# Loads of weights in parts of 112, 8 and 8 rows, in a decoder of grouped-query attention and a token mixer

## The chip, the cores and the metric

The kernel runs on one core of a Trainium2 chip. The metric is the device time of one execution in microseconds. The program is in float32 throughout, and nearly all of what it does is to stream a key and a value cache from HBM through the on-chip memory, twice over, once for each layer.

## The reference

Two layers, each of attention over a cache and of a mixer over the token axis, for two sequences of one new token. Cut to what matters:

```python
B, Sq, D = 2, 1, 512
Hq, Hkv, Sk, Dh = 32, 8, 32768, 128

def A(x, k_cache, v_cache, wq, wo):
    q = (x @ wq).reshape(B, Sq, Hq, Dh).transpose(0, 2, 1, 3)
    k = repeat(k_cache, Hq // Hkv, axis=1); v = repeat(v_cache, Hq // Hkv, axis=1)
    p = softmax(einsum("bhqd,bhkd->bhqk", q, k) * Dh ** -0.5)
    o = einsum("bhqk,bhkd->bhqd", p, v)
    return o.transpose(0, 2, 1, 3).reshape(B, Sq, Hq * Dh) @ wo

def Bmix(x, w1, b1, w2, b2):        # w1: (1, 1792), w2: (1792, 1)
    h = layernorm(x)
    u = gelu(einsum("bsd,sf->bdf", h, w1) + b1)
    return (einsum("bdf,fs->bds", u, w2) + b2).transpose(0, 2, 1)

x = A_x
for _ in range(2):                  # both layers read the same cache and weights
    x = x + A(layernorm(x), k_cache, v_cache, wq, wo)
    x = x + Bmix(layernorm(x), w1, b1, w2, b2)
```

## The kernel before

The work is cut into 32 units: layer, sequence and key head (`units`). A unit has eight chunks of 4096 keys and eight of values; a chunk is 2 MB, 16 KB in each of 128 rows (partitions). One large tile, `mem`, has thirteen cells of a chunk each. Eight of them take the stream of K and V in turn, mostly four chunks at a time (8 MB per load, 64 KB per row); in the middle of the program, where some of the last head's K and V stay on the chip for the second layer (`KEPT`, `KEPT_K`), the stream runs through three to six cells with loads of one or two chunks. Four cells, from `WCELL0` on, take weights.

The weights of a key head, its columns of `wq` and its rows of `wo` side by side, are one cell: 128 rows of 16 KB, 2 MB (`wqo[h]`). `load_weights(h, cell)` (L101) loads them with one DMA on the SP queue (L103). It is called thirteen times: once at the start for head 0, once for each of the heads 1 to 7 in the first layer, and again for the heads 0 to 4 in the second, since heads 5 to 7 (`RESIDENT`; the last of them is `keeper`) keep their cells.

All loads of K, V and weights are issued from SP, in the order that the kernel plans by hand. `stream` is a list of all loads of K and V, sorted by the chunk at which they are due; `run(t)` issues what is planned with `at(t, ...)` after chunk `t`. The weights of a unit `n` are planned ten chunks before its first chunk of K:

```python
        if n and (units[n] == (0, 0, h) or h in passing and units[n] == (1, 0, h)):
            at(kbeg[n] - 10, load_weights, h, (again if layer else weight_cell)[h])
```

They are read first by `make_q` (L238), four chunks later, and then by `out_2` (L442) after the unit's last chunk of V. A load of K (`load_k`, L272) or V (`load_v`, L352, and L346 for what stays) waits until TensorE has used up what stood in its cells: `k_chunk` (L287) computes the scores of a chunk, `v_chunk` (L391) the sum over its values. The exponentials are ACT's, the maxima and the transposes DVE's. After the last chunk of V comes a tail (`last_out`, `last_mixer`) that ends with a store of the last sequence's row in four pieces (L602); the other sequence's row is stored earlier, from ACT's queue.

Of the kernel before, what the change touches and what calls it, by code (L numbers as in the profile page):

```python
# [13 lines left out]
P = 128  # L14
# [10 lines left out]
KEPT_K = {2: 9, 4: 7, 5: 8}  # L25
KEPT = {2: (8, 6), 4: (8, 3), 5: (3, 13), 6: (8, 4), 7: (8, 5)}
REST = 3
RESIDENT = (5, 6, 7)
PIECES = (32, 16, 8, 4, 4)
THIN = 8  # L30
# [7 lines left out]
def gqa_mixer_kernel(ctx: ExitStack, tc: tile.TileContext, x, kt, v, wqo, cols, out):  # L38
# [16 lines left out]
    nc = tc.nc  # L55
# [31 lines left out]
    heads = list(range(HKV))  # L87
    passing = [h for h in heads if h not in RESIDENT]
    home = {}
    mem = const.tile([P, (WCELL0 + WCELLS) * CK + REST * QT * DH], F32, name="mem")  # L90

    def cells(k, m=1):
        return mem[:, k * CK : (k + m) * CK]
# [4 lines left out]
    def wo_at(h):  # L98
        return cells(home[h])[:, W:].rearrange("p (t c) -> p t c", t=R)

    def load_weights(h, cell):  # L101
        home[h] = cell
        nc.sync.dma_start(cells(cell), wqo[h])  # L103


    used = [0] * (WCELL0 + WCELLS + 1)
# [7 lines left out]
    def buffer(m, limit):  # L114
# [3 lines left out]
        return cells(k, m)  # L118

    load_weights(0, WCELL0)  # L120
    cols_sb = const.tile([P, 3 * FT + 1], F32, name="cols_sb")
    nc.scalar.dma_start(cols_sb, cols)
# [60 lines left out]

    *ends, keeper = RESIDENT
    assert keeper == HKV - 1 and LAYERS == 2 and B == 2
# [17 lines left out]
    def row_tile():  # L203

        return S[HALVES - 1]
# [17 lines left out]
    def unit_of(n):  # L223

        return units[n]
# [451 lines left out]
    kbeg, k_done, vbeg, v_done, t = {}, {}, {}, {}, 0  # L677
# [7 lines left out]
    def at(time, f, *a, rank=1):  # L685
        done.setdefault(time, []).append((rank, f, a))

    HC = NCH // HALVES
    weight_cell = {h: WCELL0 + h % WCELLS for h in heads}
    again = dict(zip(passing, (WCELL0 + k for k in (0, 3, 1, 2, 0))))  # L690
    for n in range(NU):
        layer, b, h = unit_of(n)
        kend, vend = k_done[n, NCH - 1], v_done[n, NCH - 1]
        ahead = v_done[n - 1, NCH - 1] if n else 0
        urgent = n in (N1, N2, NU - 1)
        if n:
            if n in (N1 + 3, N2 + 3):
                q0, q1, q2 = kbeg[n] - 1, kbeg[n] - 1, kbeg[n]
            else:
                q0 = kbeg[n] - (10 if n in (N1 + 2, N2 + 2) else 6)  # L700
                q1, q2 = q0 + 1, q0 + 2
            at(q0, make_q, n, 0)
            at(q1, make_q, n, 1)
            at(q2, make_q, n, 2)
        if n and (units[n] == (0, 0, h) or h in passing and units[n] == (1, 0, h)):
            at(kbeg[n] - 10, load_weights, h, (again if layer else weight_cell)[h])
        at(kend + 1, max_1, n)
        at(kend + 2, max_2, n)
        at(max(k_done[n, HC - 1], v_done[n - 1, HC - 1] if n else 0), turn_scores, n, 0)
        at(kend + 2, exponentials, n, 0)  # L710
        t1 = max(kend + 2, ahead + (2 if urgent else 4))
        at(t1, turn_scores, n, 1)
        at(t1, exponentials, n, 1)
        at(t1 + (1 if n == NU - 1 else 2), denominators, n)
        if n == NU - 1:
            at(t1 + 1, gelu_table)
            at(t1 + 1, last_rows, (layer, b))
            at(vend, last_out, n)
            at(vend, last_mixer, n)
            continue  # L720
        assert vbeg[n + 1] >= vend and (n + 2 >= NU or vbeg[n + 1] > vend)
        at(min(vend + 1, vbeg[n + 1]), out_1, n)
        at(vend + 2, out_2, n)
        if units[n] == lay[layer, b][-1]:
            key = (layer, b)
            at(vend, mix_1, key)
            at(vend + 2, take_rows, key, row_tile())
            at(vend + 3, mix_2, key)
            at(vend + 1, gelu_table)

            when = [vend + 3 + f for f in range(FT + 1)]
            when = [w + (w >= max(k_done[n + 1, NCH - 1] + 2, vend + 4)) for w in when]
            for f, w in enumerate(when):

                if f:
                    at(when[f - 1] + 1, hidden_out, key, f - 1, rank=0)
                if f < FT:
                    at(w, hidden_tile, key, f, rank=2)
            e = when[FT]
            at(e, take_rows, key, None, rank=2)  # L740
            at(e + 1, mix_4, key)
            if layer + 1 < LAYERS:
                at(e + 2, to_columns, key)
                assert e + 2 < kbeg[n + 3]
# [72 lines left out]
```

## Time and profile before

| | |
|---|---|
| runs of the kernel | 2515.88 us median of 3 (2515.83 to 2517.79) |
| profiled execution | 2515.91 us, its span 2514.1 us |
| PE busy | 1498.0 us (60%) |
| DVE, ACT busy | 193.1 us, 198.6 us (8% each) |
| granted TensorE clock, mean | 0.785 |
| moved by DMA | 1071.46 MB in 34802 packets, mean 426 GB/s |
| loads of weights (L103) | 13, of 2048 KB, 33.2 us from issue to landing (median) |

Engines: PE is TensorE, DVE VectorE, ACT ScalarE, POOL GpSimd, and SP the engine that issues the loads; a name with a q at its end (SPq) is the engine's sequencer, which waits and issues. L103 is line 103 of the kernel. The page gives each engine's busy time, the queues of the DMA engines with their packets and the share of sixteen engines' time that those took, and the chain of work that ended last. A load's landing is when all engines that carried it have reported.

### The profile page before, as it was taken

What the parts mean: (1) busy time and instruction counts of PE and PEld (TensorE: products, weight loads), DVE (VectorE), ACT (ScalarE), POOL (GpSimd) and SP (SyncE); (2) the same over time, 40 slices, a digit from 0 to 9 for tenths busy, and PEclk for the clock granted to TensorE, in tenths of its full rate; (3) what the DMA queues carried; (4) which work ended last, traced back from release to release, by engine and by line L of the source; (5) the groups of instructions that cost most, each with busy time, mean ns of one, the idle gap of its engine ahead of it and who ended that gap; (6) DMA issues with size and microseconds to landing.
All of it is one profiled execution on the core that took longest, in us unless ns stands there. A gap on an engine that the chain in (4) does not pass through costs nothing.

```text
span 2514.1 us, 21143 instructions
## 1 busy us (share of the span) xinstructions
PE 1498.0 (60%) x9700; PEld 413.6 (16%) x9700; DVE 193.1 (8%) x494; ACT 198.6 (8%) x582; POOL 4.9 (0%) x17
## 2 busy tenths in 40 slices
PE   4556554565546556677667676555555555566656
PEld 1111111111111111111111121111111111111112
DVE  1000000000000000011001010000000000010002
ACT  0000000000000000021000200000000000012002
POOL 0000000000000000000000000000000000000000
PEclk8777777777777778888898898777777777778878
DMA  9999999999999999999999999999999999999996
GB/s 418 434 434 431 434 432 431 433 431 437 430 431 429 432 429 430 426 421 425 427 426 427 425 421 428 433 435 435 432 433 429 432 432 433 432 430 423 432 432 280
DMA packets 34802, 1071.46 MB, mean 426 GB/s; under 512 B 4117, under 2 KB 4121, under 8 KB 4762
## 3 DMA queue, kind: packets, MB, share of 16 engines
q1 hardware_dynamic: 34424, 1070.09, 99.1%
q8 instruction: 76, 1.25, 0.2%
q14 instruction: 12, 0.10, 0.0%
q10 hardware_dynamic: 290, 0.03, 0.0%
HBM read 1070.10 MB, written 0.00 MB: 426 GB/s over the span
## 4 chain that ended last, share of the span: by engine, by line
DMA 72%; PE 27%; DVE 0%; issue 0%; ACT 0%; ACTq 0%; SPq 0%
DMA mem<-in_kt_dram 60%; PE scores L287 19%; DMA mem<-in_v_dram 12%; PE acc L391 3%; PE misc L238 3%; PE misc L429 1%; PE rows L442 1%; ACT mem L595 0%; PE misc L250 0%; PE rows L610 0%; PE misc L212 0%; ACT mem L584 0%; DVE hid L247 0%; DVE hid L365 0%; PE bcast L633 0%
## 5 line engine op out<-in xcount | busy, mean ns | idle before, releaser
L287 PE MATMUL scores<-mem,qpad 128*32 128x512 f32 x4096 | 648.1, 734 | 565.1 <-DMA mem<-in_kt_dram 564.6
L391 PE MATMUL acc<-mem,S 128*16 128x512 f32 x4092 | 618.2, 734 | 386.7 <-DMA mem<-in_v_dram 379.8
L287 PEld LDWEIGHTS scores<-mem,qpad 128*32 128x32 f32 x4096 | 142.2, 127 | 964.6 <-DMA mem<-in_kt_dram 630.1
L324 ACT ACTIVATE S<-S,neg 128x128 f32<-128x128 f32 x256 | 131.6, 518 | 1997.9 <-DVE neg L315 1524.3
L391 PEld LDWEIGHTS acc<-mem,S 128*16 128x16 f32 x4092 | 133.2, 109 | 737.2 <-issue 577.0
L238 PE MATMUL misc<-mem,xnT 128*1 128x512 f32 x256 | 122.0, 601 | 2.6 <-issue 1.6
L297 DVE TENSOR_REDUCE mx<-scores 128x1 f32<-128x512 f32 x64 | 44.3, 692 | 873.1 <-PE scores L287 853.4
L319 DVE STREAM_TRANSPOSE S<-scores 128x512 f32<-128x512 f32 x64 | 45.5, 711 | 166.8 <-PE acc L391 166.8
L621 ACT ACTIVATE hid<-bcast,bias,scale 128x512 f32<-128x512 f32 x42 | 32.7, 778 | 272.0 <-PE rows L610 136.7
L250 PE MATMUL misc<-one,hid 1*128 1x1 f32 x256 | 34.2, 250 | 33.3 <-DVE hid L247 33.3
L610 PE MATMUL rows<-hid,cols_sb 128*1 128x512 f32 x84 | 50.6, 688 | 4.1 <-ACT hid L621 4.1
L324 ACT ACTIVATION_READ_ACCUMULATOR S<-S,neg 128x1 f32 x256 | 47.8, 187 | 0.0
L429 PEld LDWEIGHTS misc<-selg,S 128*128 128x128 f32 x248 | 35.9, 223 | 44.6 <-issue 42.8
L250 PEld LDWEIGHTS misc<-one,hid 1*128 1x128 f32 x256 | 31.6, 190 | 60.6 <-DVE hid L247 48.2
L429 PE MATMUL misc<-selg,S 128*128 128x4 f32 x248 | 38.6, 279 | 0.9 <-DVE S L426 0.9
L442 PE MATMUL rows<-mem,oT 128*1 128x512 f32 x248 | 38.9, 687 | 0.0
L238 PEld LDWEIGHTS misc<-mem,xnT 128*1 128x1 f32 x256 | 21.5, 85 | 91.1 <-issue 89.9
L437 DVE TENSOR_TENSOR oT<-misc,rl 128x4 f32<-128x4 f32 x31 | 5.0, 162 | 318.3 <-PE misc L429 318.3
L426 DVE COPY S<-acc 128x512 f32<-128x512 f32 x31 | 21.4, 690 | 102.7 <-PE acc L391 102.7
L247 DVE COPY hid<-misc 1x512 f32<-1x512 f32 x32 | 21.5, 671 | 91.5 <-PE misc L238 91.5
L307 DVE TENSOR_REDUCE m<-misc 1x4 f32<-1x128 f32 x32 | 8.9, 279 | 229.6 <-PE misc L305 221.0
L422 DVE RECIPROCAL rl<-misc 128x4 f32<-128x4 f32 x32 | 5.8, 183 | 258.5 <-PE misc L420 258.5
(110 smaller groups left out, 209.9 us busy)
## 6 DMA issues: line engine op xcount, KB each, us to landing
mem<-in_kt_dram SPq DMA_DIRECT2D x60, 2048.0 KB, 12.6
mem<-in_v_dram SPq DMA_DIRECT2D x53, 2048.0 KB, 12.7
mem<-in_v_dram SPq DMA_DIRECT2D x9, 4096.0 KB, 32.5
mem<-in_kt_dram SPq DMA_DIRECT2D x7, 4096.0 KB, 28.2
mem<-in_wqo_dram SPq DMA_DIRECT2D x13, 2048.0 KB, 33.2
mem<-in_v_dram SPq DMA_DIRECT2D x4, 1280.0 KB, 21.0
mem<-in_v_dram SPq DMA_DIRECT2D x2, 768.0 KB, 23.3
mem<-in_v_dram SPq DMA_DIRECT2D x1, 1024.0 KB, 27.4
```

The source lines that it names most:

```text
L238: nc.tensor.matmul(q_ps[n][:1, :], xnT[layer, b][:, d : d + 1], wq_at(h)[:, d, :], start=(d == 0), stop=(d == DT - 1),)
L247: nc.vector.tensor_copy(q_row[n][:1, :], q_ps[n][:1, :])
L250: nc.tensor.matmul(pt[:, r : r + 1], q_row[n][:1, r * DH : (r + 1) * DH], one[:1, :], start=True, stop=True)
L287: nc.tensor.matmul(sc_ps[n, half][32 * g : 32 * g + 32, :], q, kc[:, (k * NG + g) * w : (k * NG + g + 1) * w], start=(i == 0 and k == 0), ...
L297: nc.vector.tensor_reduce(mx[n][:, half : half + 1], sc_ps[n, half], axis=AX.X, op=ALU.max)
L319: nc.vector.transpose(S[half], sc_ps[n, half])
L324: nc.scalar.activation(s[:, :, h], s[:, :, h], AF.Exp, bias=neg[n][:, h : h + 1], scale=SCALE, accum_out=lsum[n][:, half, h : h + 1],)
L391: nc.tensor.matmul(acc[32 * g : 32 * g + R * QT, :], S[half][:, col : col + R * QT], (own if q < stay else vc)[:, q * w : (q + 1) * w], st ...
L429: nc.tensor.matmul(po[:, :R], asb[:, t * DH : (t + 1) * DH], selg[:, t * R : (t + 1) * R], start=(t == 0), stop=(t == QT - 1),)
L442: nc.tensor.matmul(rows[b][32 * r : 32 * r + 1, :], oT[n][:, r : r + 1], wo_at(h)[:, r, :], start=(units[n] == lay[layer, b][0]), stop=(un ...
L610: nc.tensor.matmul(rows[key[1]][32 * g : 32 * g + 1, :], w2c[:, f : f + 1], hid[key, f], start=(f < NG), stop=(f >= FT - NG),)
L621: nc.scalar.activation(hid[key, f], px[key], AF.Gelu_apprx_tanh, bias=shift[key][:, f : f + 1], scale=slope[key][:, f : f + 1],)
```

## The change

`load_weights` takes a list of cuts, and loads the rows between each two of them with a DMA of its own. With `CUTS` these are the rows 0 to 111, 112 to 119 and 120 to 127, so that a load of weights becomes three. The planned loads use `CUTS`, but for the keeper's; the first one, of head 0 before everything else, has the default and stays whole. So eleven of the thirteen are cut: heads 1 to 6 in the first layer and 0 to 4 in the second. By the words given with the change, eight of the sixteen DMA engines then get nine rows and eight get seven, instead of eight each.

```diff
+CUTS = (0, 112, 120, 128)
...
-    def load_weights(h, cell):
+    def load_weights(h, cell, cuts=(0, P)):
         home[h] = cell
-        nc.sync.dma_start(cells(cell), wqo[h])
+        for p0, p1 in zip(cuts, cuts[1:]):
+            nc.sync.dma_start(cells(cell)[p0:p1], wqo[h, p0:p1])
...
         if n and (units[n] == (0, 0, h) or h in passing and units[n] == (1, 0, h)):
-            at(kbeg[n] - 10, load_weights, h, (again if layer else weight_cell)[h])
+            at(kbeg[n] - 10, load_weights, h, (again if layer else weight_cell)[h], (0, P) if h == keeper else CUTS)
```

Nothing else of the kernel is changed, and no other engine's instructions are.

## The prediction

> **What bounds the kernel now.** I began with the page's span, transfer and queue lines, then a table of stages, then the chain that ended last.
>
> ```profile
> span 2514.1 us, 21143 instructions
> ...
> DMA packets 34802, 1071.46 MB, mean 426 GB/s; under 512 B 4117, under 2 KB 4121, under 8 KB 4762
> ## 3 DMA queue, kind: packets, MB, share of 16 engines
> q1 hardware_dynamic: 34424, 1070.09, 99.1%
> q8 instruction: 76, 1.25, 0.2%
> ...
> q10 hardware_dynamic: 290, 0.03, 0.0%
> ...
> DMA 72%; PE 27%; DVE 0%; issue 0%; ACT 0%; ACTq 0%; SPq 0%
> ```
>
> The sixteen DMA engines are busy for 99% of the span, nearly all of it with q1, SP's loads. The table by stage (each row ends with the granted clock, the DMA share and GB/s) says that this holds in each stage and not only on average:
>
> ```profile
> 100.00:500.00 400.00, 225.39 (x1470) 63.90 (x1470) 25.14 (x64) 21.47 (x80) 0.00 (x0) 0.74 1.00 433
> 900.00:1250.00 350.00, 237.52 (x1462) 61.30 (x1458) 30.09 (x77) 37.06 (x97) 1.09 (x2) 0.84 1.00 426
> 2050.00:2480.00 430.00, 254.38 (x1662) 71.55 (x1658) 32.36 (x82) 45.99 (x119) 0.54 (x1) 0.77 1.00 430
> ```
>
> TensorE works 225 of 400 us there and otherwise waits. So the time is what the busiest DMA engine has to do, plus the tail after the last load. Whatever lengthens every load's slowest engine lengthens the kernel one for one; a microsecond on an engine that is ahead costs nothing until it is no longer ahead.
>
> The price of a row: 433 GB/s over sixteen engines is 27.1 GB/s for each, so 16 KB, one row of a weight, takes 0.605 us, and the eight rows that an engine has of such a load take 4.84 us.
>
> **The sixteen engines are not equally loaded.** The page says that 76 packets of instructions, 16 KB each, go through the same engines. I looked at short stretches of the DMA view. Each engine ends its part of a load with a 4-byte report, which is counted under "under 512 B"; sixteen such reports are one load's. The three answers below are for 627 to 629.6, 629.6 to 631.1 and 631.1 to 632.5 us, around one landing.
>
> ```profile
> DMA packets 26, 1.18 MB, mean 454 GB/s; under 512 B 8, under 2 KB 8, under 8 KB 8
> ...
> DMA packets 20, 0.85 MB, mean 568 GB/s; under 512 B 7, under 2 KB 7, under 8 KB 7
> ...
> DMA packets 8, 0.46 MB, mean 328 GB/s; under 512 B 1, under 2 KB 1, under 8 KB 1
> ```
>
> Eight engines are done early, seven come next, and one is alone at the end. The chain has that landing as the end of this piece, at 605.43 + 26.93 = 632.36 us:
>
> ```profile
> 605.43 26.93 DMA mem<-in_kt_dram
> ```
>
> Between 603 and 605.5 us one fetch of instructions went through:
>
> ```profile
> q8 instruction: 1, 0.02, 2.7%
> ```
>
> 2.7% of sixteen engines over 2.5 us is 1.08 us of one engine. The engine that came last reported about 1.3 us or more behind the seven (they are all in by 631.1). I read this as: eight of the engines share the fetches in turn, and each fetch sets its engine back by 1.08 to 1.4 us. 76 / 8 = 9.5 fetches on each make a lead of the other eight of 10.3 to 13.3 us over the whole run. The loads could end that much sooner at most, half of it by evening out.
>
> Does the lighter half get the nine rows? The change's 8-row parts go to eight engines, and a transfer of few rows uses few: the last store has four rows and, between 2512.6 and 2512.8 us, shows eight packets, four of data and four reports.
>
> ```profile
> DMA packets 8, 0.00 MB, mean 10 GB/s; under 512 B 4, under 2 KB 8, under 8 KB 8
> ```
>
> q10 counts 290 packets: two loads of 128 rows, one store of one row, and 33 reports, 16 + 16 + 1. So that one-row store ran on one engine, presumably the first of the sixteen. It ended within 2337.08 to 2337.18 us:
>
> ```profile
> DMA packets 4, 0.07 MB, mean 676 GB/s; under 512 B 2, under 2 KB 2, under 8 KB 3
> ## 3 DMA queue, kind: packets, MB, share of 16 engines
> q1 hardware_dynamic: 2, 0.07, 160.6%
> q10 hardware_dynamic: 2, 0.00, 5.8%
> ```
>
> In the same tenth of a microsecond stand a report of a load and the start of the next 64 KB row, so the store's engine finished its share of that load there. And it is an early one: 2336.7 to 2337.3 holds seven reports, the store's own and the first six of the load, and the load's other ten follow until 2339.2.
>
> ```profile
> DMA packets 15, 0.46 MB, mean 768 GB/s; under 512 B 7, under 2 KB 7, under 8 KB 8
> ...
> DMA packets 20, 0.66 MB, mean 345 GB/s; under 512 B 10, under 2 KB 10, under 8 KB 10
> ```
>
> So the first engine is of the early half, and the extra rows probably go to engines that have room.
> [...]
>
> **The change part by part.** *Rows moved.* Eleven loads take one row, 0.605 us, from eight engines and give it to the other eight: 6.7 us less on the half that sets the pace (if it is the half that fetches), 6.7 us more on the other, which was 10.3 to 13.3 us ahead. Afterwards the late half is 3.6 to 6.6 us over the plain work and the early half 6.7. By this term alone the end comes 3.6 to 6.6 us sooner.
>
> *Two more issues per load*, 22 in all. An issue of such a load takes 0.43 us on SP:
>
> ```profile
> L103 SPq DMA_DIRECT2D mem<-in_wqo_dram x13: 397/427/1339, 0.7 to 1995.3; - x13
> DMA to landing us min/median/max: 7.9/33.2/34.6
> ...
> 1994.94 0.33 SPq L352 DMA_DIRECT2D mem<-in_v_dram  x1
> 1995.32 0.43 SPq L103 DMA_DIRECT2D mem<-in_wqo_dram  x1
> 2014.43 0.33 SPq L272 DMA_DIRECT2D mem<-in_kt_dram  x1
> ```
>
> 9.4 us of SP's time, and it is free: after the issue at 1995.32 the next load is not issued until 2014.43, since it waits for a buffer. Without this cover it would be 0.86 us per load. The parts also use up two more of the eight semaphores that loads take in turn, so each load of K or V may wait for the landing of one fewer loads back; eight transfers back are still five loads, while a buffer already makes it wait for the load two back. Zero; if not, a load (4.84 us per 2 MB) once.
>
> *The reader.* A weight lands 33 us after its issue. The one issued at 701.60 (just after V's at 701.23) lands at about 734 and is first read by the L238 matmul at 759.31; some 25 us of room, and three parts on the same queues still land ahead of the next load.
>
> ```profile
> 701.23 0.33 SPq L352 DMA_DIRECT2D mem<-in_v_dram  x1
> 701.60 0.44 SPq L103 DMA_DIRECT2D mem<-in_wqo_dram  x1
> ...
> 759.31 0.85 PE misc L238 x2
> ```
>
> *The 8-row parts themselves.* In this trace every large load spreads 128 rows, and each engine writes eight rows of its own. All engines then run at the same 27.1 GB/s. Whether that speed is set at the engine or at the place in memory where it writes, the trace can't tell, since nobody else writes there. The new parts are another pattern: eight engines, one row each, into eight neighbouring partitions. At best the rows go side by side, 0.605 us a part. At worst they pass one after the other, 8 x 0.605 = 4.84 us a part, on the eight engines that have two such rows. I see no reason for a gain. No row stands between, so I take the middle, 2.72 us: such an engine then needs 7 x 0.605 + 2 x 2.72 = 9.7 us for a weight instead of 4.84, 4.85 us more, 53 us for eleven. Its lead of 10.3 to 13.3 us (11.8) takes up a part: 41.5 us later. At worst 11 x 9.1 - 10.3 = 90 us later.
> [...]
>
> **The sum.** The profiled execution took 2515.91 us, its span 2514.1 and 1.8 around it; the median of the runs is 2515.88, so a difference carries over as it is. 2515.9 + 41.5 = 2557.4 is my forecast. I take this case before the side-by-side one because the equal speed on all engines looks like a limit on the path into memory, and because the gain needs every one of the 112 + 8 + 8 rows to meet no neighbour, while one shared place is enough for the loss: the DMA engines have no idle time to hide it.
>
> **The rivals.**
> *Rows side by side* (speed set at the engines). For it: all engines have the same rate, whatever the packet. Then only the rows moved count: 3.6 to 6.6 us sooner, 2509.3 to 2512.3, nearer the first as the engine alone at the end shows the longer setback. The point that decides is a part of 0.84 us: (11.8 / 11 + 0.605) / 2, where the early half's eleven extra pieces just use up its lead. Chance 0.27, of which 0.21 below the bound of 0.2% (5.0 us, about what a measurement of this kernel can tell from no change) and 0.06 within it.
> *The extra rows go to the fetching half.* Then the slowest engines have 11 x 0.605 = 6.7 us more: 2522.6. Against it stands the one-row store in the early half. Chance 0.06.
> *It does not do what it says*: 8 rows are split over all engines, or the lead is lost at every change of stage, and nothing is evened out: 2515 to 2517. Chance 0.04.
>
> **How the numbers follow.** Rows that meet: 0.63, from 2530 (a part at 1.5 us) to 2605. Slower by over 0.2%: 0.63 + 0.06 = 0.69. Faster: 0.21. Within: 0.06 + 0.04 = 0.10. The range must reach from the side-by-side case to the meeting rows, as both signs have weight: 2508.5 to 2600, which leaves out the last of the worst case. The likeliest case's own range is 2530 to 2600.
>
> **What would show it.** If I am right, some 16 KB packets of q1 take far longer than 0.605 us after each weight's issue, the GB/s of the slices with weights drop below 430 while the DMA share stays at 1.00, and the landing of weights takes over 37 us. With rows side by side GB/s rises slightly, and the sixteen reports of a load lie closer than the 4 to 5 us around 632 us. I am wrong altogether if the time falls and single rows still take 0.605 us.

## The result, and the profile after

The changed kernel takes 2631.29 us (median of six runs, 2617.94 to 2638.52), the kernel before in the same series 2516.19. The ratio is 1.0447, 95% interval 1.043 to 1.0464: 115 us slower, where 41.5 were forecast. The sign was right; the time lies 31 us above the top of the range. The profiled execution took 2631.72 us.

The page of the changed kernel, with the lines that answer to those shown of before (each digit of the DMA row and each figure of the GB/s row is one of forty slices of the span):

```profile
span 2629.9 us, 21180 instructions
...
DMA  9999999999999999999999999999999999999996
GB/s 415 384 432 401 409 431 373 422 432 353 430 373 410 368 430 427 420 424 425 418 426 427 426 426 428 384 427 429 374 379 389 377 381 417 431 430 414 430 433 290
DMA packets 34979, 1071.47 MB, mean 407 GB/s; under 512 B 4293, under 2 KB 4297, under 8 KB 4938
...
q1 hardware_dynamic: 34600, 1070.09, 98.5%
...
DMA 74%; PE 24%; ACT 1%; DVE 0%; issue 0%; SPq 0%; POOL 0%; ACTq 0%; DVEq 0%
...
mem<-in_wqo_dram SPq DMA_DIRECT2D x11, 1792.0 KB
...
mem<-in_wqo_dram SPq DMA_DIRECT2D x2, 2048.0 KB
mem<-in_wqo_dram SPq DMA_DIRECT2D x22, 128.0 KB
```

Before, the same row of slices was level:

```profile
GB/s 418 434 434 431 434 432 431 433 431 437 430 431 429 432 429 430 426 421 425 427 426 427 425 421 428 433 435 435 432 433 429 432 432 433 432 430 423 432 432 280
```

The engines are as busy as before (98.5% of the span with q1, 99.1% before) and move the same bytes, more slowly. The dips lie in the slices with a cut load; between them about 430 stands again in most slices. The count of packets under 512 B rose from 4117 to 4293, by 176: 22 parts with eight reports each. So an 8-row part does run on eight engines.

The stages say the same (each row ends with the granted clock, the DMA share and GB/s):

```profile
100.00:500.00 400.00, 206.24 (x1324) 58.91 (x1324) 23.31 (x59) 19.38 (x72) 0.00 (x0) 0.73 1.00 411
900.00:1250.00 350.00, 232.99 (x1404) 60.54 (x1396) 28.41 (x73) 35.48 (x91) 1.08 (x2) 0.81 0.99 423
2050.00:2480.00 430.00, 239.72 (x1546) 67.49 (x1542) 30.16 (x75) 40.33 (x101) 0.54 (x1) 0.76 0.98 413
```

100 to 500 us went from 433 to 411 GB/s at a DMA share of 1.00. 900 to 1250 us, in which no cut load is planned, only from 426 to 423.

One cut load closely: the DMA view from the first 16 KB row of the first planned load to the end of its last, 84.9 to 91.7 us before and 85.1 to 101.0 us after. First before, then after:

```profile
DMA packets 173, 3.01 MB, mean 443 GB/s; under 512 B 31, under 2 KB 31, under 8 KB 31
## 3 DMA queue, kind: packets, MB, share of 16 engines
q1 hardware_dynamic: 173, 3.01, 103.7%
```

```profile
DMA packets 196, 3.64 MB, mean 229 GB/s; under 512 B 46, under 2 KB 46, under 8 KB 46
## 3 DMA queue, kind: packets, MB, share of 16 engines
q1 hardware_dynamic: 196, 3.64, 105.3%
```

A load whose rows all start within 6.8 us takes 15.9, and the stretch moves half the bytes per microsecond while no engine is idle. In the records of the single packets, from which these views are grouped, the load's rows took 0.61 us each before (0.62 at most). After, they took 1.21 on average, 116 of the 128 over 0.9 us, so most of the 112-row part's are among them. Ten took 2 to 2.5 us; they start from 93.4 us on, behind most of the others, as the 8-row parts stand in the queue. The 64 KB rows of K and V behind them suffer too: eight of them took 6.8 to 7.4 us, where 2.42 is usual. Added up, the packets of q1 took 41429 us, and 39874 before; the difference, over sixteen engines, is 97 us of the 115.

### The profile page after: what moved, and what is told of

The parts are those of the page before. It is cut to its first block, busy times and chain, and to the rows that moved or that the text cites. A ratio compares the mean times of both kernels' runs of the same rounds, so it can differ in the third digit from the quotient of the medians.

```text
span 2629.9 us, 21180 instructions
## 1 busy us (share of the span) xinstructions
PE 1521.5 (58%) x9700; PEld 421.9 (16%) x9700; DVE 193.2 (7%) x494; ACT 198.7 (8%) x582; POOL 4.9 (0%) x17
## 2 busy tenths in 40 slices
DMA packets 34979, 1071.47 MB, mean 407 GB/s; under 512 B 4293, under 2 KB 4297, under 8 KB 4938
## 3 DMA queue, kind: packets, MB, share of 16 engines
q1 hardware_dynamic: 34600, 1070.09, 98.5%
## 4 chain that ended last, share of the span: by engine, by line
DMA 74%; PE 24%; ACT 1%; DVE 0%; issue 0%; SPq 0%; POOL 0%; ACTq 0%; DVEq 0%
DMA mem<-in_v_dram 44%; DMA mem<-in_kt_dram 30%; PE acc L393 12%; PE scores L289 8%; PE misc L240 1%; PE misc L431 1%; PE rows L444 0%; ACT S L326 0%; PE misc L315 0%; PE rows L576 0%; PE misc L422 0%; PE rows L612 0%; PE misc L252 0%; PE misc L307 0%; ACT L623 0%
## 5 line engine op out<-in xcount | busy, mean ns | idle before, releaser
L289 PE MATMUL scores<-mem,qpad 128*32 128x512 f32 x4096 | 667.5, 755 | 643.1 <-DMA mem<-in_kt_dram 642.6
L240 PE MATMUL misc<-mem,xnT 128*1 128x512 f32 x256 | 125.5, 616 | 2.6 <-issue 1.6
L431 PEld LDWEIGHTS misc<-selg,S 128*128 128x128 f32 x248 | 43.0, 261 | 44.9 <-issue 42.2
L431 PE MATMUL misc<-selg,S 128*128 128x4 f32 x248 | 45.7, 307 | 0.9 <-DVE S L428 0.9
L240 PEld LDWEIGHTS misc<-mem,xnT 128*1 128x1 f32 x256 | 22.2, 88 | 96.2 <-issue 95.0
```

The source lines that it names most:

```text
L240: nc.tensor.matmul(q_ps[n][:1, :], xnT[layer, b][:, d : d + 1], wq_at(h)[:, d, :], start=(d == 0), stop=(d == DT - 1),)
L289: nc.tensor.matmul(sc_ps[n, half][32 * g : 32 * g + 32, :], q, kc[:, (k * NG + g) * w : (k * NG + g + 1) * w], start=(i == 0 and k == 0), ...
L431: nc.tensor.matmul(po[:, :R], asb[:, t * DH : (t + 1) * DH], selg[:, t * R : (t + 1) * R], start=(t == 0), stop=(t == QT - 1),)
```

## The experiments

Each starts from the kernel before. In the first seven the eleven loads that the change cuts are replaced by the lines shown.

**Is it the number of DMAs?** The load cut in three by columns, so that each part has all 128 rows:

```diff
-        nc.sync.dma_start(cells(cell), wqo[h])
+        for c0, c1 in zip(CUTS, CUTS[1:]):          # CUTS = (0, 3584, 3840, 4096)
+            nc.sync.dma_start(cells(cell)[:, c0:c1], wqo[h, :, c0:c1])
```

> The eleven loads are cut in three by columns (14 KB, 1 KB and 1 KB of each of the 128 rows) instead of by rows: as many DMAs, issues and semaphores as in the changed kernel, but every engine still writes its own eight rows. If the loss comes from rows of several engines that land near each other, this costs next to nothing: 2516 to 2519 us. If it comes from the number of DMAs (22 more issues, semaphores and reports), it loses as the change does: about 2630.

Measured 2517.88 us, ratio 1.0005 (0.9996 to 1.0015). The stage from 100 to 500 us of this kernel:

```profile
100.00:500.00 400.00, 224.94 (x1466) 63.80 (x1470) 25.14 (x64) 21.52 (x80) 0.00 (x0) 0.74 1.00 432
```

432 GB/s against 433. Issues, semaphores and three parts as such cost nothing that can be measured here (1.0 us, ratio 1.0005).

**Is it the unevenness, or the parts on eight engines?** Two cuts by rows without an 8-row part, so that no part should be left to eight engines:

```diff
-        nc.sync.dma_start(cells(cell), wqo[h])
+        for p0, p1 in zip(CUTS, CUTS[1:]):          # (0, 112, 128), and in another kernel (0, 64, 128)
+            nc.sync.dma_start(cells(cell)[p0:p1], wqo[h, p0:p1])
```

> Parts of 112 and 16 rows: sixteen engines work on each part and all have eight rows again, so nothing is uneven, and no part goes to eight engines only. If the unevenness or the eight-engine parts are what costs, this is back at 2516 to 2520. [...]

> [...] If only the uneven split costs: 2516 to 2520.

112 and 16 rows: 2606.19 us, ratio 1.035 (1.0332 to 1.0367). Two halves: 2606.45, ratio 1.036 (1.0336 to 1.0383). Both lose about 89 us with no 8-row part in them, far from the 2516 to 2520 us that were expected if the unevenness or the eight engines cost. The next kernel, whose 112 rows sixteen engines carry, still loses 72. So neither of these is the main cause; a cut by rows is. For parts of 16 and of 64 rows no count here shows the engines. The sum of the packets' times accounts for 89 us of the first and 82 of the second. In the packet records the rows of the halves took 1.18 to 1.24 us on average in the first six cut loads, about twice the 0.61 us of the uncut loads of before. Why twice was not shown.

**The 112 rows alone.** The rows 112 to 127 of the cut loads are left out (a memset at the start fills the cells):

```diff
+        nc.sync.dma_start(cells(cell)[0:112], wqo[h, 0:112])
```

> Only the part of 112 rows is loaded in the eleven loads; rows 112 to 127 of these weights are left out (zeros or an earlier head's stand there; the cells are set to zero on GpSimd at the start). It tells what the two 8-row parts cost. By my prediction's mechanism the 8-row parts are all of the loss, and this should be faster than before: 8 rows less on each of the two halves' balance, about 2505 to 2512. [...]

Measured 2588.58 us, ratio 1.0288 (1.0273 to 1.0304): 72 us slower with an eighth of these loads gone. Its packets:

```profile
DMA packets 34626, 1068.58 MB, mean 412 GB/s; under 512 B 4117, under 2 KB 4121, under 8 KB 4762
```

The reports are as many as before, 4117, so 112 rows run on all sixteen engines, seven on each by an even share; their rows took 1.01 to 1.16 us on average in the first six loads. This is the larger part of the loss, and it needs no 8-row part at all. At 0.605 us a row, seven rows instead of eight would by estimate have made the kernel some 11 x 0.605 = 6.7 us faster.

**Is it where the rows land?** Three kernels with the same source rows, issues and bytes: five parts of eight rows (rows 40 to 127 are left out, and the memset is there again). Only the place in memory differs:

```diff
+        for i in range(5):
+            nc.sync.dma_start(cells(cell)[PLACE], wqo[h, 8 * i : 8 * i + 8])
# near:   PLACE = 8 * i : 8 * i + 8
# spread: PLACE = 32 * (i // 4) + i % 4 : 32 * (i // 4) + 32 : 4
# other:  PLACE = 64 + 32 * (i // 4) + i % 4 : 96 + 32 * (i // 4) : 4
```

> The eleven loads of weights are replaced by five 8-row parts each, 40 rows of 16 KB, all in the upper eight engines' absence: eight engines, five rows each. The other 88 rows are left out (zeros or stale rows stand there). The rows land side by side, 0 to 7, 8 to 15 and so on. [...] If rows never meet, five rows take 3.0 us on eight engines and nothing on the others: near 2482, as for the next kernel.

> [...] If the reading side, the small size of a part or the eight engines are the cost, this is as slow as rows that land side by side.

> [...] If only the eight rows of a part are in each other's way, it is equal to the spread one, near 2482.

Near: 2557.94 us, ratio 1.0162 (1.0148 to 1.0176). Spread: 2497.65, ratio 0.9922 (0.9907 to 0.9937). Other: 2557.62, ratio 1.0163 (1.0149 to 1.0177). Moving the landing rows alone is worth 60 us. None of the three came out as expected. The spread kernel is 18.5 us faster (15.9 to 23.4), not the 34 to 2482: three rows fewer on each of eight engines are 11 x 3 x 0.605 = 20 us, and no lead of 10 us or more comes on top. The DMA view from 85 to 95 us, the first of these loads, in the order near, spread, other:

```profile
DMA packets 120, 2.23 MB, mean 223 GB/s; under 512 B 56, under 2 KB 56, under 8 KB 56
```

```profile
DMA packets 154, 4.57 MB, mean 457 GB/s; under 512 B 55, under 2 KB 55, under 8 KB 55
```

```profile
DMA packets 134, 3.21 MB, mean 321 GB/s; under 512 B 55, under 2 KB 55, under 8 KB 55
```

In the spread kernel all forty rows of this load took 0.61 to 0.62 us; near, mostly 1.5; other, mostly 1.2 to 1.3. So rows of one part are slowed when they land side by side, and rows that land apart are slowed too when they land in the upper 64 rows. The third kernel was the surprise: had only the rows of one part slowed each other, it would have been as good as the second. The next load differs as well: its 64 KB rows took 2.42 us beside the spread rows, and six of them 4.4 to 5.0 us beside the parts in the upper rows. Why the upper rows are slower than the lower was not shown; no trace here tells which rows an engine writes.

In the near kernel the six 64 KB rows that begin together with the parts, at 85.1 to 85.4 us, took 5.0 to 5.4 us. They are on engines that carry no part. In the spread kernel the first four parts together fill the same rows 0 to 31, and the 64 KB rows took 2.42 us. So the rows that a load fills in the end do not decide it alone: it also counts which of them are written at once. How that reaches the other engines is open. The three kernels read the same rows, so the reading side is ruled out for them. For the halves and the 112 rows the place alone was not varied.

**Had the eight engines room?** The whole load stays, and behind each of the first six follow four spread parts, into a cell that no one reads until it is rewritten: 24 rows of 0.605 us, 14.5 us more on each engine that carries them, if nothing slows them. Three more kernels do it with parts of 4, 6 and 7 rows:

```diff
         nc.sync.dma_start(cells(cell), wqo[h])
+        there = cells(WCELL0 + (h + 1) % WCELLS)    # behind the first six planned loads
+        for i in range(4):                          # ROWS = 8; 4; 6; 7
+            nc.sync.dma_start(there[i : i + 4 * ROWS : 4], wqo[h, 8 * i : 8 * i + ROWS])
```

> Before's kernel, all weights loaded whole, plus four 8-row parts (4 x 16 KB for each of eight engines) after each of the first six planned loads; they land spread, in the cell that the next weights will overwrite, and nothing reads them. They are 6 x 4 x 0.605 = 14.5 us of extra work for those eight engines. If these are the eight that are ahead by the fetches of instructions (some 1.4 us for each of about 28 fetches over eight engines until 900 us, 5 us, and more later), about two thirds of it is hidden: 2519 to 2523. If all sixteen engines were equally loaded: 2530.

> The kernel before with four further parts of 4 rows (landing 4 rows apart, in cells that no one reads until they are rewritten) behind each of the first six weight loads: the extra work is 24 rows of 16 KB at 0.605 us, 14.5 us, on each of the engines that serve a 4-row part, presumably four. The run with parts of 8 rows cost 15 us in full, so at least one of the eight engines used there has no room. If the instruction fetches (76, by eight engines in turn, 10 to 13 us on each) fall on engines none of which is among the first four, these four have that much room and the kernel takes 2518 to 2524 us. If there is no room anywhere, or the four are among the fetching engines, it takes 2530 to 2532 us.

> As the run with parts of 4 rows, with parts of 6 rows: 14.5 us more on each of six engines. If the fetches fall on the eight engines in the middle (the seventh to the fourteenth), the first six have room and the time is 2518 to 2524 us. If they begin at the fifth or sixth engine, it is 2530 to 2532 us, and the run with 4 rows stays below.

> As before, with parts of 7 rows: 14.5 us more on each of seven engines. If the fetches begin at the seventh engine, the step comes between 6 and 7 rows and this one takes 2530 to 2532 us while that with 6 stays below 2524. If they begin at the eighth, this one too stays below 2524. With no room anywhere all three take 2530 to 2532 us.

| rows in a part | us | ratio to before | interval |
|---|---|---|---|
| 8 | 2531.36 | 1.006 | 1.0047 to 1.0072 |
| 7 | 2531.65 | 1.0057 | 1.0044 to 1.0069 |
| 6 | 2531.89 | 1.0056 | 1.0043 to 1.0069 |
| 4 | 2526.22 | 1.0037 | 1.0025 to 1.005 |

With 6, 7 and 8 rows the whole 14.5 us are paid: at least one of the engines that carry the parts of 6 rows has no room. With 4 rows 9.6 us are paid (6.3 to 12.6), neither of the two cases that were expected; the six runs of this kernel lie further apart than those of the others, 2525.1 to 2531.1 us. In the packet records of the run with 8 rows the 160 rows of each of the first five such loads took 0.61 to 0.62 us, all but one; so they were not slowed, and what is paid is the work itself.

**Is a lead kept to the end?** Up to 830 us the trace of before has 23 of the 76 fetches:

```profile
q8 instruction: 23, 0.38, 0.2%
```

So the early extra of 4 rows may have met a lead of only 3 to 4 us (an estimate: 23 / 8 x 1.08 to 1.4). The same 24 rows on four engines, late, behind three loads of the second layer (eight parts each):

```diff
+        if cell != WCELL0 + h % WCELLS:             # heads 1 to 3, second layer
+            there = cells(WCELL0 + h % 3)
+            for i in range(8):
+                r = 32 * (i // 4) + i % 4
+                nc.sync.dma_start(there[r : r + 16 : 4], wqo[h, 8 * i : 8 * i + 4])
```

> The 14.5 us of extra rows on four engines again (24 rows of 16 KB, landing 4 rows apart), now late: eight parts of 4 rows behind each of three weight loads of the second layer, at about 1770 to 1950 us, in cells that no one reads until they are rewritten. The early version cost 9.6 us (6.3 to 12.6). By 830 us 23 of the 76 fetches of instructions have gone through, so the lead of the four engines could by then be 23 / 8 x 1.08 to 1.4 = 3.1 to 4.0 us; after 1650 us there are 26 more fetches. If a lead is kept through the whole run, these engines are 10 to 13 us ahead at the end, the late extra is nearly hidden, and the kernel takes 2517 to 2521 us. If the lead is lost where the loads get short in the middle of the program, only what builds up after 1650 us is there, 3.5 to 4.6 us: then 14.5 less 4 is paid, 2526 to 2528 us. With no lead at all on these engines it is 2531.

Measured 2528.74 us, ratio 1.0054 (1.004 to 1.0068): 12.3 us paid (10.1 to 17.1). These four engines have at most some 4 us of room late in the run, not 10 to 13.

The trace of before shows why. How far the first engine is ahead of the last can be read at every load, from the first of its sixteen reports to the last. That stretch is 1.0 us at the first load, 1.9 at 225, 3.4 at 545 and 4.9 at 914 to 1011 us. It then shrinks to 2.1 at 1572, is 2.5 at 1772, reaches 5.0 again at 2179 to 2217, and is 1.4 at the load that is all in by 2491. Wherever the loads are long enough to keep their reports apart, it never exceeds 5.0. The next three views each hold one load's reports, of 943.1 to 948.1, 1771.7 to 1774.35 and 2489.5 to 2491.1 us:

```profile
DMA packets 83, 2.20 MB, mean 439 GB/s; under 512 B 16, under 2 KB 16, under 8 KB 16
```

```profile
DMA packets 71, 0.95 MB, mean 359 GB/s; under 512 B 16, under 2 KB 16, under 8 KB 16
```

```profile
DMA packets 138, 0.63 MB, mean 396 GB/s; under 512 B 16, under 2 KB 16, under 8 KB 98
```

So the lead does pile up as the fetches come, 26 of them until 943 us, but it is lost again in the middle of the program, where the loads are short. In the run with the late extra the four engines that carry it, followed packet by packet, begin the first of the three loads at 1771.9 to 1772.0 us, among the first, and the last engine at 1774.35. 14.5 us less 2.4 is 12.1, and 12.3 were paid. Which of the other engines carry the fetches stays open.

## Why the prediction was wrong

*What bounds the kernel.* Right. Slower packets lengthened the kernel with the engines at a share of 0.98 to 1.00 in the stages shown. The tail did not grow: the span ends 23.6 us after the last 16 KB row, 23.8 before. The reader of the weights (now L240) had its room; it waited 2.6 us in all, 1.6 of it for its own issue (busy and mean ns | idle before, and what ended it):

```profile
L240 PE MATMUL misc<-mem,xnT 128*1 128x512 f32 x256 | 125.5, 616 | 2.6 <-issue 1.6
```

*Two more issues per load, and their semaphores.* Right at zero: the cut by columns has them all and costs 1.0 us (ratio 1.0005).

*The 8-row parts.* Right in kind, and near in size: 2.72 us was taken, and the longest rows of the first cut load, ten of 128, took 2 to 2.5 us. Neighbouring rows do slow each other: mostly 1.5 us a row side by side, in the near kernel, and 0.61 to 0.62 four apart, in the spread one. Cutting the last 16 rows into two eights costs 2631.3 - 2606.2 = 25 us. Against the 112 rows alone the two parts add 43 us; the sum's 11 x 2 x 2.72 = 60 less its lead of 11.8 would be 48. That this is so near is partly luck, since there is no such lead.

*The 112 rows.* This is the step that failed. They were put at 7 x 0.605 us, as if undisturbed. With them alone the rows took 1.01 to 1.16 us and the kernel was 72 us slower. The sum asked where the rows of the 8-row parts land, and not where these do. Why rows are slowed at seven to an engine that are not at eight was not shown.

*Only the load's own rows are late.* The sum took each engine's rows of the weight and nothing behind them. The 64 KB rows behind them took up to three times their 2.42 us. So the bound "at worst 90 us" was none.

*The lead.* Wrong. Fetches of 1.08 to 1.4 us were read about rightly (the 76 packets took 0.89 to 1.17 us each), but their sum over the run, 10.3 to 13.3 us, is not there to be used. The reports of single loads, already in the trace of before, lie at most 5.0 us apart and 1.4 at the end. 14.5 us of undisturbed extra rows cost 15.2 on the eight engines, and 9.6 or 12.3 on four, and the spread kernel's gain leaves no place for one of that size. The reading from the one-row store, that its engine is early, says nothing of seven more engines, and no trace here shows that it is the first of the sixteen or one of those that the parts use. So by these runs, even with rows that don't meet, the cut would have gained nothing and cost up to 6.7 us: the rival in which the extra rows go to the fetching half (2522.6, chance 0.06) was nearer than "rows side by side" (0.27). "The lead is lost at every change of stage", a clause of the last rival, comes nearest to what the trace shows.

*What would show it.* The signs named came: long 16 KB packets, slices below 430 GB/s at a full DMA share, and a landing past 37 us (the first cut load's last row ends at 101.0 us, 43 us after its issue at 57.8).

Of the 115 us, 72 stand with the 112 rows alone; the other 16 rows in one part make it 89, in two parts 115. The 97 us that the lengthened packets account for leave 18 us open. No mechanism was shown that gives these sizes. No version came out that beats the kernel before. The spread kernel is faster only because it leaves rows out.

## What to carry to other kernels

Where the DMA engines bind, as here, load all 128 rows in one DMA, and if a load must be cut, cut it by columns: three parts then cost nothing that could be measured (1.0 us), while the three cuts by rows that were tried cost 3.5% to 4.5%. Before moving work between DMA engines, ask where each row lands, and try it: here two placings of the same forty rows lay 60 us apart. A balance of counts says nothing of that. A lead read from one short stretch should be followed through the whole trace, load by load, and tried with a known extra load on those engines, before a gain is built on it.

## What was not expected of the hardware

The cut loads slowed their neighbours in the queue as well as themselves: behind the first of them eight 64 KB rows took 6.8 to 7.4 us instead of 2.42. Spreading forty rows four apart, instead of side by side, moved the kernel by 60 us, and the same rows landing in the upper 64 rows gave all of it back (2557.94, 2497.65 and 2557.62 us side by side, spread and in the upper rows). And 112 rows, on all sixteen engines (4117 reports, as before), are no substitute for 128: without the last sixteen the kernel is 2.9% slower than with them in one load.
